# Parallel FNet and MLP on one core: a new order of the front, of four row stores and of one block's output columns

## The chip, the cores and the metric

The kernel runs on one core of one Trainium2 chip. The metric is the time of one execution on the device in microseconds (us), as the median of several runs. Before the change that is 851.08 us (three runs, 850.71 to 851.48). All matrices are 32-bit floats in and out.

## What is computed

For one sequence of S = 2048 rows and D = 640 columns, with F = 1536 hidden units:

```python
xn = _layernorm(x, axis=-1)
# _A_ref: real part of a Fourier transform along both axes
a = jnp.einsum("bsd,ed->bse", xn, dft_hid_re)
b = jnp.einsum("bsd,ed->bse", xn, dft_hid_im)
y = jnp.einsum("ts,bse->bte", dft_seq_re, a) - jnp.einsum("ts,bse->bte", dft_seq_im, b)
# _B_ref: a two-layer MLP
h = _gelu(jnp.einsum("bsd,df->bsf", xn, w1) + b1)
z = jnp.einsum("bsf,fd->bsd", h, w2) + b2
return x + y + z
```

## The kernel before, in words

**Products.** Every matrix product keeps nearly full precision by splitting both operands: a number is a high part, written by ScalarE as `fp32r` (L160), plus a low part, which VectorE computes as the difference (L161). One logical product is then three TensorE matmuls of 128x128 weights by 128x512 columns: high by high, high by low, low by high (L278 to L280, and L304 for the first layer of the MLP, where the three are the kinds `(0, 0)`, `(0, 1)`, `(1, 0)` of a chunk `j` of the 640 columns).

**Order.** The program is written out by hand: instructions stand on each engine in the order in which the code issues them, and nothing reorders them. An instruction whose input is late therefore holds all that stands behind it on its engine. DMAs are issued by SyncE (queue SP), by ScalarE (only the loads of two row chunks at the start, and the last stores) and by GpSimd (queue POOL).

**Stages.** The 2048 rows are four blocks of 512, each of four chunks of 128 rows. First the MLP of blocks 0 and 1: for each of 12 hidden units (of 128 columns) `hidden(g)` forms the hidden values in one PSUM bank, `gelu(g, acc)` activates and splits them, `output(g)` multiplies them by `w2` into five PSUM banks. `hidden` runs two units ahead of `output`. Beside it `first_block(i)` and `second_block(i)` normalize the later row chunks, store them to the scratch tensor `xs` in DRAM (`ln_apply`, L199 to L203), read them back by block (`load_z`) and turn them with VectorE; `prep_w` builds the Fourier weights and stores them to `wit` in DRAM from GpSimd's queue (L418). Then the MLP of blocks 2 and 3 runs with a scheme of sums that saves multiplications (`head`, `mid`, `finish`), then the Fourier transform.

**The front (L657 to L772).** The first four row chunks aren't normalized before their products: they are only centered, and the scale is multiplied in later. For chunk c, `x[c]` is loaded, its mean is found (VectorE's `ln_stats` for chunks 0 and 2, ScalarE's `sum_on_act` for 1 and 3), and `center` (L705, VectorE) or a ScalarE activation (L716, chunk 1) writes `xp[:, c]`. `transpose_x` (L693) turns 128x128 pieces of `xp` on TensorE into the PSUM banks `tacc[j]`, and `split` evicts each bank into `XTT` (tile `xtt`, high by ScalarE L160, low by VectorE L161). The weights of hidden unit 0 arrive in two pieces (columns 0 to 255 and 256 to 639) and are split at L728 and L729; those of unit 1 are loaded in two cuts of four DMAs each and split by `prep_w1(1)`. Before the transposes TensorE runs `NWARM` = 10 warm-up matmuls on a tile of zeros (L676), which VectorE clears (L665) and casts to `fp32r` (L667); one more stands between the transposes of chunks 1 and 2. `hidden(0)` takes its 15 matmuls in the order `FIRST`.

**The boundary after block 1 (from L1135).** The five output banks of block 1 are moved out by `outs`: for each of five column groups `e`, ScalarE adds the bias in the bank (L368), VectorE turns it into a scratch tile (L371), GpSimd adds it to the tile `xo` (L373). The banks so freed are what `mid(0)`, `head(1)` and `finish(0)` of the next stage need: `copy_bank` (L857) writes one of them, the bank sums (L452 on `banks` and `fifth`) two. `forms_s3` ends with a subtraction on `zs`, the split of one set of weight sums (`tw`), a load of the next, and one more form (`hs`), all ahead of `outs(1, (0,))`; `rest`, called inside `mid(0)` after its bank copy, moves out the other four column groups.

Of the kernel before, what the change touches and what calls it, by code (L numbers as in the profile page):

```python
# [15 lines left out]
P = 128  # L16
Q = 4
B = 32
EPS = 1e-5
NWARM = 10  # L20
# [6 lines left out]
def kernel(  # L27
# [171 lines left out]
    def ln_apply(c, eng=nc.vector):  # L199
        m = MV[:, c % 4]  # L200
        eng.tensor_scalar(xt[c], xt[c], m[:, 0:1], m[:, 3:4], op0=ALU.subtract, op1=ALU.mult)
        for k in range(NC):
            nc.sync.dma_start(xs[c % NC * NC + k, c // NC * B : (c // NC + 1) * B], xt[c][k * B : (k + 1) * B])  # L203
# [85 lines left out]

    def hidden(g, aside=None):  # L290
# [4 lines left out]
        if g == 0:  # L295
            steps = FIRST
        if g == 1:

            steps.sort(key=lambda s: s[1] == 2)
# [10 lines left out]
    FIRST = [(0, 0), (0, 2), (1, 0), (1, 2), (0, 1), (2, 0), (2, 2), (1, 1), (3, 0), (3, 2)]  # L310
    FIRST += [(2, 1), (4, 0), (4, 2), (3, 1), (4, 1)]
# [353 lines left out]
    nc.vector.memset(zeros, 0.0)  # L665
    warm = whole["as"][:, :TB]
    nc.vector.tensor_copy(warm, zeros)  # L667
# [3 lines left out]
    load_w1(1, cuts=(0, 2, ND))  # L671
# [3 lines left out]
    def warm_up():  # L675
        nc.tensor.matmul(wacc, warm[:, :P], warm, start=True, stop=True)  # L676
# [3 lines left out]
    load_w1(2)  # L680
# [41 lines left out]
    center(2, ALU.subtract, MV[:, 2, 0:1])  # L722
    sum_on_act(3)
    center(3, ALU.add, MV[:, 3, 5:6], 0, 2)
    center(3, ALU.add, MV[:, 3, 5:6], 2, ND)
    for lo, hi in ((0, 2 * P), (2 * P, D)):
        h, l = (W1[0][:, k, lo:hi] for k in range(2))
        nc.scalar.activation(h, first_w1[:, lo:hi], AF.Copy)  # L728
# [13 lines left out]
    acc0 = hidden(0)  # L742
    prep_w1(1)
    acc1 = hidden(1)
# [239 lines left out]
    def second_block(i):  # L984
# [8 lines left out]
        if i == 2:  # L993
            ln_scale(12, 4)
            for c in range(12, 16):
                ln_apply(c)
# [138 lines left out]
    outs(1, (0,), yt=lambda n: AB[:, 0], done=False)  # L1135
# [665 lines left out]
```

## Time and profile before

| what | us |
|---|---|
| median of three runs | 851.08 |
| the profiled execution | 850.46 |
| its span in the trace | 848.7 |
| TensorE busy in the span | 841.7 |
| VectorE busy | 666.8 |
| ScalarE busy | 356.0 |
| GpSimd busy | 48.9 |

The span runs from the first to the last instruction of the program; 1.76 us of the profiled execution lie around it. PE is TensorE's matmuls and PEld its weight loads, DVE is VectorE, ACT is ScalarE, POOL is GpSimd, SP is SyncE. A row of a timeline reads: start, duration, engine, line, operation, what is written from what is read with the shapes, count, and in brackets the idle time before it and what ended it. Matmuls overlap, so a matmul's duration is longer than the distance to the next one.

### The profile page before, as it was taken

How to read it: one execution, taken by the hardware profiler on the slowest of the kernel's cores; microseconds unless marked ns; L12 is line 12 of the kernel's file. 1: busy time of each engine (PE TensorE's matmuls, PEld its weight loads, DVE VectorE, ACT ScalarE, POOL GpSimd, SP SyncE). 2: the span in 40 equal slices, each digit the busy share in tenths (PEclk: the TensorE clock that was granted, in tenths of full speed). 3: DMA queues.
4: the chain of work that ended last, by engine and by line, in shares of the span. 5: the costliest groups of instructions: out<-in, count | busy, mean ns of one | idle time of the engine just before them, and what ended most of it. 6: DMA issues, size and time to landing. Idle time of an engine off the chain costs nothing.

```text
span 848.7 us, 10340 instructions
## 1 busy us (share of the span) xinstructions
PE 841.7 (99%) x3707; PEld 695.2 (82%) x3707; DVE 666.8 (79%) x841; ACT 356.0 (42%) x499; POOL 48.9 (6%) x70
## 2 busy tenths in 40 slices
PE   9999999999999999999999999999999999999997
PEld 7888888878888888888888888888888888888886
DVE  6665766776758888779988887889967898885687
ACT  7454534456665555343444344232323433223241
POOL 0000311031221400000000000000000000000001
PEclk9999999999999999999999999999999999999999
DMA  6667699837679989858644679663865779705464
GB/s 182 192 184 188 159 228 252 193 87 189 202 245 355 358 186 174 173 132 188 152 137 111 162 229 289 151 150 98 205 168 169 253 191 229 306 19 180 124 172 108
DMA packets 207491, 158.45 MB, mean 187 GB/s; under 512 B 81040, under 2 KB 180880, under 8 KB 206928
## 3 DMA queue, kind: packets, MB, share of 16 engines
q1 hardware_dynamic: 198752, 135.25, 62.7%
q0 software_dynamic: 4144, 21.24, 6.3%
q10 hardware_dynamic: 4544, 1.31, 0.6%
q8 instruction: 29, 0.48, 0.3%
q14 instruction: 22, 0.18, 0.1%
HBM read 114.76 MB, written 42.99 MB: 186 GB/s over the span
## 4 chain that ended last, share of the span: by engine, by line
PE 99%; DVE 0%; issue 0%
PE banks L278 29%; PE banks L279 29%; PE banks L280 29%; PE banks L304 10%; PE banks L676 1%; PE banks L693 0%; PE banks L336 0%; PE banks L339 0%; PE banks L337 0%; DVE yo L1766 0%; DVE zeros L665 0%; DVE as L667 0%; PE banks L764 0%
## 5 line engine op out<-in xcount | busy, mean ns | idle before, releaser
L278 PE MATMUL banks<-as,xab 128*128 128x512 f32 x411 | 159.9, 389 | 0.0
L280 PE MATMUL banks<-as,xab 128*128 128x512 f32 x411 | 159.9, 389 | 0.0
L279 PE MATMUL banks<-as,xab 128*128 128x512 f32 x411 | 159.9, 389 | 0.0
L160 ACT ACTIVATE as<-r 128x1024 fp32r<-128x1024 f32 x80 | 85.0, 1062 | 178.1 <-PE banks L280 149.7
L161 DVE TENSOR_TENSOR as<-r,as 128x1024 fp32r<-128x1024 f32 x80 | 97.2, 1216 | 41.5 <-ACT as L160 41.5
L278 PEld LDWEIGHTS banks<-as,xab 128*128 128x128 f32 x411 | 77.1, 188 | 16.1
L279 PEld LDWEIGHTS banks<-as,xab 128*128 128x128 f32 x411 | 77.1, 188 | 16.0
L280 PEld LDWEIGHTS banks<-as,xab 128*128 128x128 f32 x411 | 77.1, 188 | 16.0
L278 PE MATMUL banks<-as,xc 128*128 128x512 f32 x224 | 87.1, 389 | 0.0
L279 PE MATMUL banks<-as,xc 128*128 128x512 f32 x224 | 87.1, 389 | 0.0
L280 PE MATMUL banks<-as,xc 128*128 128x512 f32 x224 | 87.1, 389 | 0.0
L160 ACT ACTIVATE as<-rt 128x1024 fp32r<-128x1024 f32 x32 | 34.0, 1062 | 70.5 <-PE banks L280 62.5
L304 PE MATMUL banks<-xtt,xab 128*128 128x512 f32 x240 | 57.1, 391 | 0.0
L304 PEld LDWEIGHTS banks<-xtt,xab 128*128 128x128 f32 x240 | 44.7, 188 | 9.8 <-ACT xtt L160 0.4
L278 PEld LDWEIGHTS banks<-as,xc 128*128 128x128 f32 x224 | 42.0, 188 | 8.8
L279 PEld LDWEIGHTS banks<-as,xc 128*128 128x128 f32 x224 | 42.0, 188 | 8.7
L280 PEld LDWEIGHTS banks<-as,xc 128*128 128x128 f32 x224 | 42.0, 188 | 8.7
L161 DVE TENSOR_TENSOR as<-rt,as 128x1024 fp32r<-128x1024 f32 x32 | 38.8, 1211 | 5.3 <-ACT as L160 5.3
L160 ACT ACTIVATE as<-u 128x1024 fp32r<-128x1024 f32 (+1 forms) x24 | 22.1, 920 | 48.2 <-PE banks L280 48.2
L512 DVE STREAM_TRANSPOSE r<-raw 128x1024 f32<-128x1024 f32 x32 | 39.5, 1240 | 3.1 <-PE banks L280 2.6
L161 DVE TENSOR_TENSOR as<-u,as 128x1024 fp32r<-128x1024 f32 (+1 forms) x24 | 24.9, 1042 | 18.8 <-ACT as L160 18.8
L512 DVE STREAM_TRANSPOSE rt<-raw 128x1024 f32<-128x1024 f32 x32 | 38.8, 1230 | 0.9 <-PE banks L280 0.8
(352 smaller groups left out, 1618.5 us busy)
## 6 DMA issues: line engine op xcount, KB each, us to landing
raw<-in_A_dft_seq_re_dram SPq DMA_DIRECT2D x64, 256.0 KB, 5.6
raw<-in_A_dft_seq_im_dram SPq DMA_DIRECT2D x64, 256.0 KB, 5.0
ws<-wit SPq DMA_DIRECT2D x15, 384.0 KB, 5.4
xs<-x SPq DMA_DIRECT2D x64, 80.0 KB, 1.8
xo<-in_A_x_dram SPq DMA_DIRECT2D x16, 320.0 KB, 6.7
xab<-wit SPq DMA_DIRECT2D x13, 384.0 KB, 4.2
wit<-wstp POOLq DMA_DIRECT2D x12, 384.0 KB, 3.7
x<-in_A_x_dram SPq DMA_DIRECT2D x14, 320.0 KB, 4.4
```

What stands on the lines that cost most here:

```text
L160: nc.scalar.activation(h, s, AF.Copy)
L161: nc.vector.tensor_tensor(l, s, h.bitcast(F32), op=ALU.subtract)
L278: nc.tensor.matmul(acc, wh, mh, start=first, stop=False, skip_group_check=goes_on)
L279: nc.tensor.matmul(acc, wh, ml, start=False, stop=False, skip_group_check=goes_on)
L280: nc.tensor.matmul(acc, wl, mh, start=False, stop=last, skip_group_check=goes_on)
L304: nc.tensor.matmul(acc, W1[i][:, a, j * P : (j + 1) * P], XT[j][:, b], start=n == 0, stop=n == len(steps) - 1)
L512: nc.vector.transpose(held(pieces[g][2], u).rearrange("p c (n i) -> p c n i", i=B), r.rearrange("p n (c i) -> p c n i", i=B))
L676: nc.tensor.matmul(wacc, warm[:, :P], warm, start=True, stop=True)
```

## The change

**Warm-ups.** VectorE clears 128x128 zeros and casts nothing; 13 warm-ups of 128x128 by 128x128 in plain fp32 take the place of 10 of 128x512 in `fp32r`.

**The first transposes and products.** ScalarE, not VectorE, centers the first two column chunks of row chunk 3 (the fourth), before it takes the first weight piece. VectorE centers chunk 2 in two pieces (columns chunks 0 to 1, then 2 to 4). The second weight piece is split after the first two evictions. TensorE takes the last three transposes of chunk 3 after the first two products; `first_two` also interleaves the first matmuls of unit 1 with the last of unit 0. Unit 1's weights are loaded uncut, unit 2's in two cuts.

TensorE at the front (`as` and `zeros` are the warm-up tiles, `ident,xp` the transposes, `xtt,xab_122` and `xab_123` products of units 0, 1 and 2), before and now:

```order
L676 MATMUL banks<-as 128x512 x10
L693 MATMUL banks<-ident,xp 128x128 x10
L676 MATMUL banks<-as 128x512
L693 MATMUL banks<-ident,xp 128x128 x10
L304 MATMUL banks<-xtt,xab_122 128x512 x30
```

```order
L692 MATMUL banks<-zeros 128x128 x13
L709 MATMUL banks<-ident,xp 128x128 x10
L692 MATMUL banks<-zeros 128x128
L709 MATMUL banks<-ident,xp 128x128 x7
L304 MATMUL banks<-xtt,xab_122 128x512 x2
L709 MATMUL banks<-ident,xp 128x128 x3
L304 MATMUL banks<-xtt,xab_122 128x512 x28
```

Three transposes have moved behind two products; the number of transposes and products is the same.

ScalarE at the front, from the sum of chunk 3 (`ab,mv<-x_120`) to unit 1's weights (the last row of each), before and now:

```order
L699 ACTIVATE ab,mv<-x_120 128x640
L728 ACTIVATE xab_122<-w1r_139 128x256
L728 ACTIVATE xab_122<-w1r_139 128x384
L160 ACTIVATE xtt<-banks 128x512 x5
L160 ACTIVATE xab_122<-w1r_148 128x640
```

```order
L715 ACTIVATE ab,mv<-x_120 128x640
L745 ACTIVATE xp<-x_120,mv 128x4x2x32
L742 ACTIVATE xab_122<-w1r_138 128x256
L160 ACTIVATE xtt<-banks 128x512 x2
L742 ACTIVATE xab_122<-w1r_138 128x384
L160 ACTIVATE xtt<-banks 128x512 x3
L160 ACTIVATE xab_122<-w1r_147 128x640
```

One centering of 256 columns is new on ScalarE, and two evictions stand ahead of the second weight piece.

**Block 3's stores.** In `second_block(2)` the stores of chunks 12 and 13 go out from GpSimd's queue, those of 14 and 15 still from SyncE's.

**Block 1's columns.** The end of `forms_s3` becomes `forms_ob` and is called after `outs(1, (0,))`; column groups 2 and 1 are moved out before `mid(0)`, groups 3 and 4 still inside it. ScalarE at this boundary, from the two forms of `s3` to the two of `s4` (`b2c` marks the biases of `outs`, `banks<-banks` alone the bank copy of `mid(0)`), before and now:

```order
L160 ACTIVATE xtt<-zs 128x512 x2
L160 ACTIVATE tw_1549<-rq_1424 128x1024
L160 ACTIVATE hs<-zs 128x512
L368 ACTIVATE banks<-banks,b2c 128x512
L857 ACTIVATE banks<-banks 128x512
L368 ACTIVATE banks<-banks,b2c 128x512 x4
L160 ACTIVATE xtt<-zs 128x512 x2
```

```order
L160 ACTIVATE xtt<-zs 128x512 x2
L386 ACTIVATE banks<-banks,b2c 128x512
L160 ACTIVATE tw_1570<-rq_1427 128x1024
L160 ACTIVATE hs<-zs 128x512
L386 ACTIVATE banks<-banks,b2c 128x512 x2
L881 ACTIVATE banks<-banks 128x512
L386 ACTIVATE banks<-banks,b2c 128x512 x2
L160 ACTIVATE xtt<-zs 128x512 x2
```

The first bias is ahead of two splits, and two more are ahead of the bank copy. On VectorE the only move there is that the turn of the first column group (into `ab`) stands ahead of the subtraction on `zs`, the split of `tw` and the form in `hs`; the other four turns stay where they were.

The diff, cut to its core:

```diff
-NWARM = 10
+NWARM = 13
...
-    def ln_apply(c, eng=nc.vector):
+    def ln_apply(c, queue=nc.sync):
...
-            nc.sync.dma_start(xs[c % NC * NC + k, c // NC * B : (c // NC + 1) * B], xt[c][k * B : (k + 1) * B])
+            queue.dma_start(xs[c % NC * NC + k, c // NC * B : (c // NC + 1) * B], xt[c][k * B : (k + 1) * B])
...
+    def first_two():
+        kinds = ((0, 0), (0, 1), (1, 0))
+        second = sorted(((j, k) for j in range(ND) for k in range(3)), key=lambda s: s[1])
+        order = [(0, s) for s in FIRST[:13]] + [(1, s) for s in second[:2]]
+        order += [(0, FIRST[13]), (1, second[2]), (0, FIRST[14])] + [(1, s) for s in second[3:]]
+        for n, (g, (j, k)) in enumerate(order):
+            if n == 2:
+                transpose_x(3, 2, ND)
+                for e in range(2, ND):
+                    split(XT[e][:, 0], XT[e][:, 1], tacc[e])
+                prep_w1(1)
+            a, b = kinds[k]
+            ends = FIRST if g == 0 else second
+            nc.tensor.matmul(
+                bank(g),
+                W1[g][:, a, j * P : (j + 1) * P],
+                XT[j][:, b],
+                start=(j, k) == ends[0],
+                stop=(j, k) == ends[-1],
+            )
+        return bank(0), bank(1)
...
-    FIRST = [(0, 0), (0, 2), (1, 0), (1, 2), (0, 1), (2, 0), (2, 2), (1, 1), (3, 0), (3, 2)]
-    FIRST += [(2, 1), (4, 0), (4, 2), (3, 1), (4, 1)]
+    FIRST = [(0, 0), (0, 2), (1, 0), (1, 2), (0, 1), (2, 0), (1, 1), (3, 0), (2, 2), (3, 2)]
+    FIRST += [(4, 0), (4, 2), (2, 1), (3, 1), (4, 1)]
...
-    nc.vector.memset(zeros, 0.0)
-    warm = whole["as"][:, :TB]
-    nc.vector.tensor_copy(warm, zeros)
+    nc.vector.memset(zeros[:, :P], 0.0)
...
-    load_w1(1, cuts=(0, 2, ND))
+    load_w1(1)
...
-        nc.tensor.matmul(wacc, warm[:, :P], warm, start=True, stop=True)
+        nc.tensor.matmul(wacc[:, :P], zeros[:, :P], zeros[:, :P], start=True, stop=True)
...
-    load_w1(2)
+    load_w1(2, cuts=(0, 2, ND))
...
-    center(2, ALU.subtract, MV[:, 2, 0:1])
     sum_on_act(3)
-    center(3, ALU.add, MV[:, 3, 5:6], 0, 2)
-    center(3, ALU.add, MV[:, 3, 5:6], 2, ND)
-    for lo, hi in ((0, 2 * P), (2 * P, D)):
+
+    def split_first(lo, hi):
         h, l = (W1[0][:, k, lo:hi] for k in range(2))
         nc.scalar.activation(h, first_w1[:, lo:hi], AF.Copy)
         nc.vector.tensor_tensor(l, first_w1[:, lo:hi], h.bitcast(F32), op=ALU.subtract)
+
+    nc.scalar.activation(
+        chunked(xp[:, 3])[:, :, :2],
+        xt[3].rearrange("p (q c i) -> p q c i", q=Q, i=B)[:, :, :2],
+        AF.Identity,
+        bias=MV[:, 3, 5:6],
+    )
+    center(2, ALU.subtract, MV[:, 2, 0:1], 0, 2)
+    center(2, ALU.subtract, MV[:, 2, 0:1], 2, ND)
+    split_first(0, 2 * P)
+    center(3, ALU.add, MV[:, 3, 5:6], 2, ND)
     transpose_x(0, 0, ND)
     transpose_x(1, 0, ND)
     warm_up()
-    for j0, j1 in ((0, 2), (2, ND)):
-        transpose_x(2, j0, j1)
-        transpose_x(3, j0, j1)
-    for j in range(ND):
+    transpose_x(2, 0, 1)
+    transpose_x(3, 0, 2)
+    transpose_x(2, 1, ND)
+    for j in range(2):
         split(XT[j][:, 0], XT[j][:, 1], tacc[j])
+    split_first(2 * P, D)
...
-    acc0 = hidden(0)
-    prep_w1(1)
-    acc1 = hidden(1)
+    acc0, acc1 = first_two()
...
-                ln_apply(c)
+                ln_apply(c, nc.gpsimd if c < 14 else nc.sync)
...
+
+    def forms_ob():
         add(two(2), two(2), ZT, ALU.subtract)
         split_w1(1)
         load_rq(2)
...
     outs(1, (0,), yt=lambda n: AB[:, 0], done=False)
-
-    def rest():
-        free = (4, 5, 0, 1)
-        outs(1, (2, 1, 3, 4), yt=lambda n: A["zs"][:, free[n] * TB : (free[n] + 1) * TB])
-
+    forms_ob()
+    outs_at((2, 1), (4, 5))
     mid(0, rest)
```

`outs_at(order, free, done=False)` calls `outs(1, order, ...)` with scratch tiles `free` of `zs`, and the new `rest` is `outs_at((3, 4), (0, 1), done=True)`.

More of the change, by code (lines that the diff above doesn't have):

```diff
@@ L294, in hidden @@
         steps = [(j, k) for j in range(ND) for k in range(3)]
[L295 to L299, printed above, removed]
         for n, (j, k) in enumerate(steps):
@@ L1133, with outs_at, rest @@
     oacc[3] = [bank(k) for k in (5, 6, 7, 3, 4)]
+    def outs_at(order, free, done=False):
+        outs(1, order, yt=lambda n: A["zs"][:, free[n] * TB : (free[n] + 1) * TB], done=done)
+    def rest():
+        outs_at((3, 4), (0, 1), done=True)
     outs(1, (0,), yt=lambda n: AB[:, 0], done=False)
-    def rest():
-        free = (4, 5, 0, 1)
-        outs(1, (2, 1, 3, 4), yt=lambda n: A["zs"][:, free[n] * TB : (free[n] + 1) * TB])
+    forms_ob()
+    outs_at((2, 1), (4, 5))
     mid(0, rest)
```

2 lines of the change are left out of this document (1 added, 1 removed).

## Prediction

> **What bounds the kernel now.** I read the page first, then the chain that ended last, then the timeline of one engine at a time for the first 20 us and for 174 to 188 us.
>
> ```profile
> span 848.7 us, 10340 instructions
> PE 841.7 (99%) x3707; PEld 695.2 (82%) x3707; DVE 666.8 (79%) x841; ACT 356.0 (42%) x499; POOL 48.9 (6%) x70
> PE 99%; DVE 0%; issue 0%
> L278 PE MATMUL banks<-as,xab 128*128 128x512 f32 x411 | 159.9, 389 | 0.0
> ```
>
> TensorE is busy for 99% of the span and is 99% of the chain, and its groups have 0.0 us idle before them. An edit can therefore pay in two ways only: the products begin sooner, or a hole between products closes. TensorE in the front:
>
> ```profile
> 1.91 4.63 PE L676 MATMUL banks<-as 128*128 128x512 f32 x10 [1.91 <-DVE as L667]
> 6.42 1.98 PE L693 MATMUL banks<-ident,xp 128*128 128x128 f32 x10
> 8.16 0.48 PE L676 MATMUL banks<-as 128*128 128x512 f32 x1
> 8.48 1.25 PE L693 MATMUL banks<-ident,xp 128*128 128x128 f32 x10
> 9.66 7.46 PE L304 MATMUL banks<-xtt,xab 128*128 128x512 f32 x31
> 23.99 3.56 PE L304 MATMUL banks<-xtt,xab 128*128 128x512 f32 x15
> ```
>
> Ten warm-ups, ten transposes, a spare warm-up, ten transposes, then products from 9.66. A product in a full stream costs (3.56 - 0.39) / 14 = 0.226 us. The first 31 should take 30 x 0.226 + 0.39 = 7.17 and take 7.46, so waits inside them cost about 0.3.
>
> The speed of TensorE changes in the front (window, its length, PE busy and count, PEld, granted clock, DMA share, GB/s; line L693 alone):
>
> ```profile
> 6.40:7.70 1.30, 1.28 (x6) 1.30 (x7) 1.00 0.24 62
> 8.45:9.60 1.15, 1.12 (x10) 1.01 (x9) 1.00 0.28 72
> ```
>
> The same transpose takes 1.30 / 6 = 0.217 us before 7.7 and 1.15 / 10 = 0.115 after. The granted clock reads 1.00 in both, so the step is seen only in the spacing: TensorE reaches full speed about 5.8 us after its first matmul.
>
> **The front: what feeds the first product.** ScalarE, VectorE and the weight loads:
>
> ```profile
> 0.91 0.48 DVE L665 MEMSET zeros<- 128x512 f32 x1 [0.91 <-PEq L1787]
> 6.56 0.74 ACT L699 ACTIVATE ab<-x 128x640 f32<-128x640 f32 x1 [0.15 <-DMA x<-in_A_x_dram]
> 7.20 0.19 ACT L699 ACTIVATION_READ_ACCUMULATOR ab<-x 128x1 f32 x1
> 7.30 0.40 ACT L728 ACTIVATE xab<-w1r 128x256 fp32r<-128x256 f32 x1
> 7.38 1.15 DVE L705 TENSOR_SCALAR xp<-x,mv 128x640 f32<-128x640 f32 x3
> 8.47 0.53 ACT L728 ACTIVATE xab<-w1r 128x384 fp32r<-128x384 f32 x1 [0.77 <-DMA w1r<-in_B_w_dram]
> 9.01 2.56 ACT L160 ACTIVATE xtt<-banks 128x512 fp32r<-128x512 f32 x5
> 9.65 0.30 PEld L304 LDWEIGHTS banks<-xtt,xab 128*128 128x128 f32 x2 [0.16 <-ACT xtt L160]
> 12.42 0.74 ACT L160 ACTIVATE xab<-w1r 128x640 fp32r<-128x640 f32 x1 [0.86 <-DMA w1r<-in_B_w_dram]
> 13.21 3.48 PEld L304 LDWEIGHTS banks<-xtt,xab 128*128 128x128 f32 x16 [0.25 <-ACT xab L160]
> ```
>
> The first product waits for the first eviction (9.01, product at 9.66: 0.65 later). That eviction stands behind the second weight piece, for which ScalarE idles 0.77. The change moves that piece behind two evictions and gives ScalarE the first 256 columns of chunk four (a 128x256 activation, 0.40).
>
> *ScalarE's side.* Centering runs from 7.39 to 7.8, the first weight piece to 8.2, so an eviction can start at 8.25: a product at 8.9. On VectorE the three centerings of row 7.38 lose a quarter of their columns and wait behind one weight subtraction; they end near 8.9, before the three late transposes need them. The second piece then starts at 9.3, later than its landing at 8.47, and stream and evictions keep 0.1 us apart up to bank four. I cost it at nothing; the cover is those first six products, and a miss costs about 0.1.
>
> *TensorE's side.* The cast goes and the memset shrinks to a quarter. Its cost isn't shown: between 0.12 (a quarter of 0.48) and 0.48; I take 0.2, nearer the quarter, so warm-ups start at 1.15, not 1.91. There are 13 of fp32 128x128, a form that the trace lacks. The nearest rows are the slow fp32 transposes (0.217) and the slow 128x512 warm-ups ((6.42 - 1.91) / 10 = 0.45). I take 0.45, as the operation is a multiplication, not a transpose, and keep 0.217 for the range. The block then ends at 1.15 + 13 x 0.45 = 7.0: 0.6 *after* the chunk-0 transposes began before. The Trainium skill, "FP8 and Floating Point Precision", TensorE Precision Notes, says that true FP32 takes four passes through the array; four passes of 128 columns are the 512 of the old warm-up, which gives the 0.45 too, and no run here shows it yet.
>
> With full speed again 5.8 us after the first matmul (6.95): ten transposes at 0.115 to 8.15, the spare to 8.5, two transposes and their drain to 8.85, product 0.65 later at 9.5. The new order puts waits there: behind the first two products stand the last three transposes, and the evictions of banks two to four wait for those, so a late first product would hold them too. Three transposes (0.35) now stand inside the stream, so it stands where one begun at 9.85 would: 0.2 worse than 9.66. Against that, weights of block one come by four loads and not eight, and the wait at 13.21 (PEld 0.25, of which about 0.1 reaches PE, as a 0.19 load is partly covered) goes; fewer waits on the first evictions may give 0.1 more. Sum: 0.
>
> If full speed comes before about 5.5, the block ends in time, transposes start at 6.42 and run at 0.115 throughout: 7.6, the spare 7.9, two more and drain 8.25. That meets ScalarE's 8.25: product at 8.9, equivalent start 9.25, gain 0.4, plus 0.1 at 13.2: 0.5. The three timed runs of before lie 0.77 apart, as much as this whole difference, so I don't count on one fixed moment. I take **0.2** of 0 to 0.5. What is late next is ScalarE's chain of squares and spread; it starts with the weights of block one, which land sooner, and moves along.
>
> **The boundary at 174 to 188 us.**
>
> ```profile
> 174.26 1.29 DVE L161 TENSOR_TENSOR xtt<-zs,xtt 128x512 fp32r<-128x512 f32 x2 [0.88 <-ACT xtt L160]
> 178.34 0.71 DVE L371 STREAM_TRANSPOSE ab<-banks 128x512 f32<-128x512 f32 x1
> 179.15 0.58 ACT L857 ACTIVATE banks<-banks 128x512 f32<-128x512 f32 x1 [2.38 <-DVE ab L371]
> 179.49 0.39 PE L280 MATMUL banks<-xc,xab 128*128 128x512 f32 x1
> 179.78 0.50 PE L278 MATMUL banks<-xtt,tw 128*128 128x512 f32 x1
> 180.33 2.51 DVE L371 STREAM_TRANSPOSE zs<-banks 128x512 f32<-128x512 f32 x4 [1.28 <-ACT banks L368]
> 181.13 5.49 POOL L373 TENSOR_TENSOR xo<-xo,zs 128x512 f32<-128x512 f32 x4 [0.65 <-DVE zs L371]
> 182.77 1.26 DVE L452 TENSOR_TENSOR banks<-banks,fifth 128x512 f32<-128x512 f32 x2
> 183.79 0.39 PE L280 MATMUL banks<-r,tw 128*128 128x512 f32 x1
> 184.09 0.50 PE L278 MATMUL banks<-r,tw 128*128 128x512 f32 x1
> 183.94 3.23 DVE L161 TENSOR_TENSOR xtt<-zs,xtt 128x512 fp32r<-128x512 f32 x2
> 186.94 0.39 PE L278 MATMUL banks<-xtt,xab 128*128 128x512 f32 x1
> 187.22 0.50 PE L279 MATMUL banks<-xtt,xab 128*128 128x512 f32 x1
> ```
>
> Three holes. From 179.49 to 179.78 is 0.29, 0.06 over a step; that product lasts 0.50, not 0.39, as its weights couldn't load ahead, 0.11 more: 0.17 each, 0.51 in all. The first hole waits for the bank copy at 179.15, which waits for the transpose of 178.34, which stands on VectorE behind three long instructions. The change puts the transpose ahead of them and two bias activations ahead of the copy: copy ready near 178.8, hole closed, **0.17** sure.
>
> The second waits for the bank sums (182.77 to 184.03), the third for the forms from 183.94. The 1.28 idle before 180.33 goes, so the sums come 1.28 sooner, less what GpSimd's earlier add takes from VectorE. Price: two subtractions cost 1.29 alone and 3.23 beside GpSimd's adds (2.7 us of overlap), 0.72 per us; the moved add lasts 5.49 / 4 = 1.37: 1.0. Net 0.3 sooner, 183.7, while TensorE, 0.17 ahead, needs the sums at 183.85. Both holes close or stay by 0.1; half of 0.34 is **0.17**. The Trainium skill, "SBUF — State Buffer", SBUF: two separate sides, speaks against it: a GpSimd operation and a VectorE operation with two SBUF inputs exclude each other for a whole instruction. Its full block of one add would leave the sums at 184.0 and both holes open: 0.17 for the boundary in place of 0.34.
>
> **Block 3's stores.** Eight of sixteen go from SyncE to GpSimd.
>
> ```profile
> 128.61 0.54 POOL L418 DMA_DIRECT2D wit<-wst x1 [5.23 <-DVE wst L161]
> 132.72 10.72 SPq L203 DMA_DIRECT2D xs<-x  x16
> 136.77 1.34 ACT L160 ACTIVATE wst<-wt 128x256 fp32r<-128x256 f32 x4 [4.36 <-DVE wt L396]
> 154.45 1.25 DVE L786 STREAM_TRANSPOSE zt<-z 128x1024 f32<-128x1024 f32 x1 [2.88 <-DMA z<-xs]
> ```
>
> At 0.54 an issue they hold GpSimd 4.3 us, and the weight write of 128.61 stands behind them, some 2.5 us later. ScalarE reuses that buffer at 136.77 after 4.36 us of idle: covered, and without the cover ScalarE loses the excess, not TensorE, which has no hole there. SyncE is through 5 us sooner, and the 2.88 wait at 154.45 goes. TensorE didn't wait for it: **0**.
>
> **Rivals.** *A, full speed early:* the front gives 0.5, the boundary 0.34 to 0.51: 850.1 and below. The trace's 5.8 us speaks against, the spread for it. The Trainium skill, "TensorE: Matmul & The Clock Gate", Part 1, says that activity is judged in free-running windows of 3.4 us, so release moves from run to run; the 5.8 us fits. *B, no change:* the block holds the transposes, the front loses 0.2 to 0.4, the boundary gives it back: 851.1. For it: 7.0 against 6.42. *C, slower:* the 13 small matmuls cost more than 0.45, as each loads its own weights. Each 0.1 moves the front by 1.3; with half of the old block's 0.39 weight load uncovered (0.64 each) transposes start at 9.5, the front loses 2.7: 853.4. It passes 0.2% from about 0.57 each. Nothing shows such loads uncovered. *D, too short:* at 0.217 the block ends at 4.0, TensorE stands still for 2.4 us and products run slow to about 12.2 (6.42 + 5.8): half of 2.3 us and slow transposes, 1.5 lost, 852.3.
>
> **How the numbers follow.** The sum is -0.2 - 0.34 = -0.54. The profiled execution took 850.46 (span 848.7 plus 1.76 around it), which gives 849.9; the median of before is 0.62 above it, and on that footing the forecast is 851.08 - 0.54 = **850.5**. Chances: forecast (850.2 to 850.9) 0.48, A 0.2, B 0.2, C 0.06, D 0.06. The range runs from A's low end (849.5) to 852.1, short of C and part of D. 0.2%, about what a measurement can tell from no change, is 1.7 us: everything shown to be at stake is 0.5 + 0.51, so faster has 0.03, slower 0.06 (C, the top of D), the same 0.91.
>
> **What would show it.** Right: first warm-up near 1.15, ten transposes from 6.4 to 7.0, first product between 8.9 and 9.5, no PEld wait at the first product of block one, no hole near 179.8. Wrong: transposes starting after 7.2, products 0.43 apart after 10 us, holes still at 184.1 and 187.2, ScalarE idle on a weight write near 137, or any new hole in TensorE.

## The result, and the profile after

The changed kernel takes 852.87 us (median of 15 runs, 851.15 to 853.93), the kernel before beside it on the same chips 850.84 (15 runs, 850.3 to 851.7): a ratio of 1.0023, 95% interval 1.0016 to 1.003. It is slower by 2.0 us, where 850.5 and "the same" were forecast; 852.87 lies above the range. The profiled execution took 852.07 us, its span 850.3: 1.6 more than before.

The page of the profile after, in the order in which the lines of before were read (span, busy time with the number of instructions, chain by engine, the first group):

```profile
span 850.3 us, 10378 instructions
PE 842.7 (99%) x3724; PEld 696.8 (82%) x3724; DVE 666.6 (78%) x840; ACT 356.0 (42%) x500; POOL 54.0 (6%) x78
PE 86%; DVE 4%; DMA 3%; ACT 3%; SPq 2%; issue 2%; POOL 0%; ACTq 0%; POOLq 0%; DVEq 0%
L278 PE MATMUL banks<-as,xab 128*128 128x512 f32 x411 | 160.0, 389 | 0.5 <-DVE zs L389 0.5
```

TensorE's busy time rose by only 1.0, yet it is 86% of the chain where it was 99%: other engines now stand on the path for a part of the way. And there are 17 more matmuls and 17 more weight loads (x3724 for x3707), though the code issues only 3 matmuls more.

The front, TensorE's timeline of the kernel after; the last line is the first product of unit 0's output, and below it the same place before:

```profile
1.05 5.67 PE L692 MATMUL banks<-zeros 128*128 128x128 f32 x26 [1.05 <-DVE zeros L683]
6.56 1.25 PE L709 MATMUL banks<-ident,xp 128*128 128x128 f32 x10
8.94 0.73 PE L304 MATMUL banks<-xtt,xab 128*128 128x512 f32 x2
9.76 6.70 PE L304 MATMUL banks<-xtt,xab 128*128 128x512 f32 x28
20.19 0.39 PE L354 MATMUL banks<-hs,rt 128*128 128x512 f32 x1
```

```profile
20.59 0.39 PE L336 MATMUL banks<-hs,rt 128*128 128x512 f32 x1
```

The 13 fp32 warm-ups stand as x26: each is two instructions, about 0.21 us apart. The front does gain: at 20 us TensorE is 0.4 ahead (20.59 - 20.19). So the loss comes later. Two new groups of holes in TensorE, near 150 us and near 182 us:

```profile
148.32 1.29 PE L322 MATMUL banks<-xtt,as 128*128 128x512 f32 x5
149.82 0.50 PE L278 MATMUL banks<-hs,r 128*128 128x512 f32 x1 [0.20 <-ACT hs L344]
150.89 0.50 PE L279 MATMUL banks<-hs,r 128*128 128x512 f32 x1 [0.57 <-DVE hs L346]
151.23 0.39 PE L280 MATMUL banks<-hs,r 128*128 128x512 f32 x1
...
182.71 0.50 PE L278 MATMUL banks<-as,xab 128*128 128x512 f32 x1 [0.46 <-DVE zs L389]
```

With 0.226 a product, the five of 148.32 end their steps at 149.45; the next starts at 149.82, then 150.89, then 151.23: 0.37 + 0.84 + 0.11 = 1.3 us lost to the activation `hs`. Between 176 and 200 us the holes make 1.12 (0.73 of it at 182.71), before 0.52. The balance: -0.4 + 1.3 + 0.6 = 1.5 of the 1.6.

ScalarE makes `hs`. Its rows ahead of the hole, after, and the same activation before:

```profile
145.55 0.42 ACT L160 ACTIVATE wst<-wt 128x256 fp32r<-128x256 f32 x1 [3.41 <-DMA wit<-wst]
147.91 0.62 ACT L160 ACTIVATE wst<-wt 128x256 fp32r<-128x256 f32 x2 [1.74 <-DMA wit<-wst]
148.43 0.67 ACT L340 ACTIVATE ab<-banks,b1c 128x512 f32<-128x512 f32 x1
```

```profile
143.85 0.67 ACT L322 ACTIVATE ab<-banks,b1c 128x512 f32<-128x512 f32 x1
```

The activation is 4.6 us later, behind two waits for weight writes to DRAM. Going back along the engines, the first place where the two executions part is VectorE at 78 us. Before, then after:

```profile
78.63 0.71 DVE L238 STREAM_TRANSPOSE zt<-z 128x512 f32<-128x512 f32 x1 [0.60 <-DMA z<-xs]
105.75 0.89 DVE L185 BATCH_NORM_STATS2 st<-x 128x6 f32<-128x320 f32 x2 [0.54 <-DMA x<-in_A_x_dram]
```

```profile
79.48 0.71 DVE L238 STREAM_TRANSPOSE zt<-z 128x512 f32<-128x512 f32 x1 [1.79 <-DMA z<-xs]
107.02 0.89 DVE L185 BATCH_NORM_STATS2 st<-x 128x6 f32<-128x320 f32 x2 [2.22 <-DMA x<-in_A_x_dram]
109.08 0.89 DVE L185 BATCH_NORM_STATS2 st<-x 128x6 f32<-128x320 f32 x2 [0.92 <-DMA x<-in_A_x_dram]
```

VectorE reached the transpose 0.3 sooner and then waited 1.79 for the read of block 1's rows, not 0.60. SyncE issued that read 0.4 sooner (69.71, before 70.08), and its last quarter landed 9.6 us after the first issue (79.36), not 8.4 (78.51). The changed lines do not touch this read.

### The profile page after: what moved, and what is told of

Read it like the earlier page. It is cut to its first block, busy times and chain, and to the rows that moved or that the text cites. A ratio compares the mean times of both kernels' runs of the same rounds, so it can differ in the third digit from the quotient of the medians.

```text
span 850.3 us, 10378 instructions
## 1 busy us (share of the span) xinstructions
PE 842.7 (99%) x3724; PEld 696.8 (82%) x3724; DVE 666.6 (78%) x840; ACT 356.0 (42%) x500; POOL 54.0 (6%) x78
## 4 chain that ended last, share of the span: by engine, by line
PE 86%; DVE 4%; DMA 3%; ACT 3%; SPq 2%; issue 2%; POOL 0%; ACTq 0%; POOLq 0%; DVEq 0%
PE banks L279 27%; PE banks L278 27%; PE banks L280 27%; PE banks L322 3%; DMA wit<-wst 1%; DMA z<-xs 1%; PE banks L304 1%; SPq L406 1%; DMA xs<-x 1%; PE banks L692 1%; SPq L203 0%; ACT ab L340 0%; DVE r L161 0%; DVE zt L238 0%; DVE st L185 0%
## 5 line engine op out<-in xcount | busy, mean ns | idle before, releaser
L322 PE MATMUL banks<-xtt,xab 128*128 128x512 f32 x210 | 50.1, 390 | 0.0
L322 PEld LDWEIGHTS banks<-xtt,xab 128*128 128x128 f32 x210 | 39.3, 188 | 8.3 <-DVE xab L161 0.2
```

The source lines that it names most:

```text
L322: nc.tensor.matmul(acc, W1[i][:, a, j * P : (j + 1) * P], XT[j][:, b], start=n == 0, stop=n == len(steps) - 1)
```

## The experiments

All times are medians; "before" was run beside each group (850.66 to 850.79). The ratio is an estimate of its own with its interval and need not be the quotient of two medians. A profile shows one execution of a kernel, not its median.

| run | us | ratio to before, 95% |
|---|---|---|
| e1 stores only | 851.26 | 1.0006 (0.9997 to 1.0015) |
| e2 the change without the stores | 852.16 | 1.0019 (1.0011 to 1.0028) |
| e3 front only | 852.98 | 1.0031 (1.0019 to 1.0042) |
| e4 columns only | 850.60 | 1.0001 (0.9992 to 1.001) |
| e5 front, 5 long warm-ups | 850.40 | 0.9996 (0.9987 to 1.0004) |
| e6 before, 34 more instructions | 852.66 | 1.0018 (1.0009 to 1.0027) |
| e7 whole change, 5 long warm-ups | 850.87 | 1.0001 (0.9993 to 1.001) |
| e8 e7 without the stores | 850.16 | 0.999 (0.9982 to 0.9999) |
| e9 before, 34 more, later | 851.39 | 1.0007 (0.9999 to 1.0016) |
| e10 before, 110 more, small warm-ups | 856.22 | 1.0061 (1.0048 to 1.0073) |
| e11 e7, stores behind the weight writes | 849.93 | 0.9989 (0.998 to 0.9997) |
| e12 e7, later reads | 850.06 | 0.9992 (0.9983 to 1.0001) |
| e13 before, 5 products halved | 850.88 | 1.0003 (0.9994 to 1.0011) |
| e14 before, 11 halved | 852.13 | 1.002 (1.0011 to 1.0029) |
| e15 before, 17 halved | 853.00 | 1.0025 (1.0015 to 1.0035) |
| e16 before, 55 halved | 853.46 | 1.0022 (1.0012 to 1.0032) |

### Which part loses (e1 to e4)

e1, the stores alone (on the kernel before):

```diff
-                ln_apply(c)
+                ln_apply(c, nc.gpsimd if c < 14 else nc.sync)
```

> The kernel before with one edit: chunks 12 and 13 are stored to xs from GpSimd's queue. Theory W (weight writes): the stores push back GpSimd's weight writes to wit, ScalarE waits for their landing before it reuses the buffer, its activations of hidden values slip, and TensorE gets a hole near 150 us and late banks near 182: 1.5 to 2.6 us slower than before, holes only behind 149 us. Rival C (columns): the cost of the whole change sits in the new order at the boundary, and the stores alone cost under 0.5. Rival F (front): the front costs in most executions, the stores alone nothing.

e2, the change with this line put back:

```diff
-                ln_apply(c, nc.gpsimd if c < 14 else nc.sync)
+                ln_apply(c)
```

> The changed kernel with all of block 3's stores back on SyncE's queue. Theory W: the loss is gone and the front's gain is left, 0.2 to 0.8 under before, no hole near 150. Rival C: still 0.5 to 1.5 above before, with the hole near 182. Rival F: still 1 to 2 above before.

e3, the kernel before with the new front alone (warm-ups, centering, `first_two`, weight cuts). Against the whole change it takes back the line of e2, and at the boundary, where `forms_s3` gets the lines of `forms_ob` again and `rest` all four groups:

```diff
-    outs(1, (0,), yt=lambda n: AB[:, 0], done=False)
-    forms_ob()
-    outs_at((2, 1), (4, 5))
+    outs(1, (0,), yt=lambda n: AB[:, 0], done=False)
```

> The kernel before with the change's front alone. Theory W and rival C: 0.2 to 0.5 under before, the products from 8.9 us. Rival F: 1 to 2 above before, with the products later than 9.7 in the slower executions.

e4, the kernel before with the columns alone:

```diff
+    def forms_ob():
         add(two(2), two(2), ZT, ALU.subtract)
...
+    forms_ob()
+    outs_at((2, 1), (4, 5))
     mid(0, rest)
```

> The kernel before with the new order of block 1's columns alone. Theory W: 0.1 to 0.4 under before, the holes at 179.8, 184.1 and 187.2 (0.51 in all) down to 0.3 or less. Rival C: 0.5 to 1.5 above before, with a new hole of 0.7 or more near 181, where the next stage's first bank waits for a transpose that stands behind a split slowed by GpSimd's add. Rival F: no difference over 0.2.

The front alone loses 2.3 us; the stores alone 0.5, which the interval does not resolve; the columns nothing. So Theory W and Rival C are out as the main cause. Rival F has the right part but not the right way: in e3 the products begin as early as in the whole change (8.81), and its profile loses the time far behind them, 0.9 us near 136, 0.2 near 157 and 1.7 near 180 us.

Theory W's path exists, though. e1's profiled execution is its slowest (853.47 of 850.61 to 853.47), and in it TensorE has the hole of the changed kernel near 150 us, while VectorE's wait for the read at 70 us is that of before (0.59):

```profile
150.85 0.51 PE L278 MATMUL banks<-hs,r 128*128 128x512 f32 x1 [0.35 <-ACT hs L326]
151.93 0.50 PE L279 MATMUL banks<-hs,r 128*128 128x512 f32 x1 [0.57 <-DVE hs L328]
```

e2, with the late read and without the stores, has no hole there in its profile and loses 1.3 near 182 us. So the hole near 150 us comes with the stores; what the front alone costs shows near 180 us, and in e3 near 136 us too.

Why the columns gain nothing in e4 stands in its rows (VectorE, GpSimd, TensorE), with the split of `tw` before below them:

```profile
174.77 1.28 DVE L161 TENSOR_TENSOR xtt<-zs,xtt 128x512 fp32r<-128x512 f32 x2
177.71 2.31 DVE L161 TENSOR_TENSOR tw<-rq,tw 128x1024 fp32r<-128x1024 f32 x1
180.55 2.50 DVE L371 STREAM_TRANSPOSE zs<-banks 128x512 f32<-128x512 f32 x4
```

```profile
176.82 2.12 POOL L373 TENSOR_TENSOR xo<-xo,ab 128x512 f32<-128x512 f32 x1 [21.93 <-DVE ab L371]
```

```profile
181.30 0.50 PE L278 MATMUL banks<-as,xab 128*128 128x512 f32 x1
```

```profile
176.61 1.22 DVE L161 TENSOR_TENSOR tw<-rq,tw 128x1024 fp32r<-128x1024 f32 x1
```

The hole before `xtt,tw` is gone, but GpSimd's add now stands beside the split of `tw`, which takes 2.31 where it took 1.22. The four transposes start at 180.55 (before 180.33), and the first product on `as` at 181.30 waits for them: 0.06 and 0.11, a hole of the size of the one that was closed. The other two stay. Holes from 176 to 200 us: 0.56, before 0.52. But VectorE also came to this stretch later in e4: it begins the split into `xtt` at 174.77, before at 174.26. From there to the four transposes it took 5.78, before 6.07, so the new order is 0.29 quicker. In e7 below, with the same order at the boundary, VectorE came in time:

```profile
173.98 1.29 DVE L161 TENSOR_TENSOR xtt<-zs,xtt 128x512 fp32r<-128x512 f32 x2 [0.80 <-ACT xtt L160]
179.77 2.50 DVE L389 STREAM_TRANSPOSE zs<-banks 128x512 f32<-128x512 f32 x4
```

The holes from 176 to 200 us are 0.27 there, and 0.22 in the profiles of e11 and e12. So the columns do gain about 0.3 where VectorE isn't late; a median of e4 can't resolve that.

### What in the front loses (e5 to e8)

Nothing in the front touches the read at 70 us. What reaches it is TensorE's instruction stream. The page's section on DMA queues has a queue of its own for code; the line is the same before and after but for its share:

```profile
q8 instruction: 29, 0.48, 0.2%
```

29 packets of 16 KB, one about every 29 us, and TensorE has 2 x 3724 = 7448 instructions: 257 a packet. That they are TensorE's code is inferred from this, and from what follows. With 34 more instructions at the front every later fetch comes some 34 / 256 x 29 = 3.9 us sooner; the one that concerns us came 4.0 sooner (80.46, after 76.42). (The Trainium skill, "Runtime: NRT & Kernel Launch", Instruction fetch mechanics, says the same size: blocks of 16 KiB, 256 instructions, fetched by the sequencer's own DMA queue; the count agrees. It calls the cost of a crossing "mostly hidden": TensorE itself has no hole at this fetch, but the runs below show a cost to the transfer beside it.) The fetch of this queue before, in the window from 79.6 to 81.5 us, and after, from 76 to 78 us (packets, MB, share of 16 engines):

```profile
q8 instruction: 1, 0.02, 3.3%
```

```profile
q8 instruction: 1, 0.02, 4.3%
```

Before, it falls behind the read (landed 78.51); after, into it. *Theory I*: the fetch delays the transfer that it meets, and VectorE waits. e5 takes the new front (e3) but makes the warm-ups long and few, e7 does it to the whole change, e8 to the change without the stores:

```diff
-NWARM = 13
+NWARM = 5
...
-    nc.vector.memset(zeros[:, :P], 0.0)
+    nc.vector.memset(zeros[:, : 5 * P // 2], 0.0)
...
-        nc.tensor.matmul(wacc[:, :P], zeros[:, :P], zeros[:, :P], start=True, stop=True)
+        nc.tensor.matmul(wacc[:, :n], zeros[:, :P], zeros[:, :n], start=True, stop=True)
```

with `n` 320. e6 does the opposite: the kernel before, with 34 more instructions for the same columns (21 warm-ups of 256 for 10 of 512, and six products of unit 1 in two halves):

```diff
-NWARM = 10
+NWARM = 21
...
+            cuts = (0, TB // 2, TB) if g == 1 and 3 <= n < 9 else (0, TB)
```

> The front alone once more, but with 5 warm-ups of 128x320 in fp32 in place of 13 of 128x128: nearly the same time on TensorE and two TensorE instructions more than before the change, not 34 (each fp32 matmul shows as two). Theory I (instruction fetch): TensorE's code comes in blocks of 16 KB, one for each 256 instructions; 34 more instructions bring each block some 4 us earlier, into the last part of block 1's read (z) and the load of chunks 12 to 15, and everything that hangs on those is late at 180 us. Then this kernel is 0.2 to 0.6 under before, with a fetch near 80 us. Rival D (earlier weight loads): the front's earlier loads and products themselves collide with the reads; then it stays 1.5 to 2.5 above before, as the front alone did.

> The kernel before with 34 TensorE instructions more and the same work: 21 warm-ups of 128x256 in place of 10 of 128x512, and six products of hidden unit 1 cut into two halves of 256 columns. Theory I: 1.5 to 2.5 above before, a fetch near 76 us, the last part of block 1's read landing 9.4 to 9.8 us after its first issue and not 8.4. Rival D: within 0.4 of before, as no load moved.

> The whole change with 5 warm-ups of 128x320. Theory I: the stores' 0.5 and the front's gain are left, 850.5 to 851.4; rival D: 852.3 to 853.3, as the change.

> Front and block 1's columns without the stores on GpSimd, with 5 warm-ups of 128x320. Theory I: 0.3 to 0.8 under before, the best of all so far. Rival D: 1 to 2 above before, as the change without the stores.

All four times lie in Theory I's ranges and outside Rival D's. In e6's profile the fetch comes at 77.06 and the read's last quarter lands 9.6 us after the first issue, as asked. Each pair that differs in these instructions differs by about 2 us: e3 and e5 by 2.6, the whole change and e7 by 2.0, e2 and e8 by 2.0, e6 and the kernel before by 1.9. VectorE at 78 us in e5, then in e6:

```profile
78.36 0.71 DVE L238 STREAM_TRANSPOSE zt<-z 128x512 f32<-128x512 f32 x1 [0.35 <-DMA z<-xs]
```

```profile
79.93 0.71 DVE L238 STREAM_TRANSPOSE zt<-z 128x512 f32<-128x512 f32 x1 [1.75 <-DMA z<-xs]
```

So the loss belongs to the additional instructions, not to what the front computes: e6 has none of the change. e6's profiled execution was one of its quick ones (851.08 of 850.4 to 853.96): VectorE is late in it, and little of that reached TensorE (nothing up to 230 us, 0.4 behind it).

TensorE's five long warm-ups in e5, which the last part needs (x10, as each fp32 matmul shows as two):

```profile
1.25 5.70 PE L692 MATMUL banks<-zeros 128*128 128x320 f32 x10 [1.25 <-DVE zeros L683]
```

### Place of the fetch, or number of instructions? (e9, e10, e13 to e16)

e9 puts the same 34 behind the read, into the hidden units at 88 to 95 us; e10 puts 110 ahead of it, partly by small warm-ups:

```diff
+            cuts = (0, TB // 2, TB) if g == 12 and 3 <= n < 12 or g == 13 and 3 <= n < 11 else (0, TB)
```

```diff
-NWARM = 10
+NWARM = 32
...
-        nc.tensor.matmul(wacc, warm[:, :P], warm, start=True, stop=True)
+        nc.tensor.matmul(wacc[:, :n], warm[:, :P], warm[:, :n], start=True, stop=True)
...
+            cuts = (0, TB // 2, TB) if g in (1, 2, 3) and 3 <= n < 14 else (0, TB)
```

(`n` of the warm-ups is 160.)

> The kernel before, with the same 34 more instructions on TensorE as the sixth experiment, but later: 17 products of the hidden units at 88 to 95 us are taken in two halves of 256 columns. Theory I (a block of TensorE's code is fetched while the read of block 1's rows is under way, 70 to 78 us): here the fetch at 80.5 us stays where it is and only those from 108 us on come about 3.9 us sooner, so the last piece of that read lands 8.2 to 8.5 us after its issue as before, and the time is 850.4 to 851.2. Rival I-b (the later fetches, near 105 and 132 us, do the harm): last piece unchanged, time 852 to 853, holes between 135 and 190 us. Rival II (the number of instructions itself costs): 852 to 853 too, but with the lost time at the halved products.

> The kernel before, with 110 more instructions on TensorE for the same columns, all ahead of 28 us: 32 warm-ups of 160 columns for 10 of 512, and 33 products of hidden units 1 to 3 in two halves. The fetch of 80.5 us should come near 68 us, ahead of the read of block 1's rows (from 70.1 us), and the one of 135.7 near 123, inside the read of block 2's rows (121.7 to 130.7 us). Theory I (what counts is whether a fetch falls into a read, not how many instructions there are): the last piece of the first read lands 8.2 to 8.5 us after issue although there are three times as many extra instructions as in the sixth experiment; the last piece of the second read comes at 9.8 to 10.5 in place of 9.0; time 850.3 to 851.5 if that second read has slack, up to 852.5 if not. Rival II (each extra instruction costs): 856 or more, as the sixth experiment lost 1.9 with a third of them.

e9: the read's last piece comes 8.2 us after issue, and the time is 851.39, above the 851.2 that Theory I allowed and below what the rivals asked. Its interval (0.9999 to 1.0016) does not exclude that nothing changed. Most of the loss goes with the fetch near 77. About 0.26 of the 0.6 that is left is the price of the halved products themselves (two hidden units took 7.06, before 6.80); whether the later fetches cost the rest isn't settled. In e9's profile VectorE waits for the rows of chunks 12 to 15 (1.04 and 0.56) and TensorE has one hole of 1.1 at 180 us; but e5 has such waits too (1.89 and 0.79) and no such hole. VectorE in e9, then in e5:

```profile
106.42 0.89 DVE L185 BATCH_NORM_STATS2 st<-x 128x6 f32<-128x320 f32 x2 [1.04 <-DMA x<-in_A_x_dram]
108.11 0.89 DVE L185 BATCH_NORM_STATS2 st<-x 128x6 f32<-128x320 f32 x2 [0.56 <-DMA x<-in_A_x_dram]
```

```profile
106.98 0.89 DVE L185 BATCH_NORM_STATS2 st<-x 128x6 f32<-128x320 f32 x2 [1.89 <-DMA x<-in_A_x_dram]
108.91 0.89 DVE L185 BATCH_NORM_STATS2 st<-x 128x6 f32<-128x320 f32 x2 [0.79 <-DMA x<-in_A_x_dram]
```

e10 was a poor experiment: its time is set by its own warm-ups.

```profile
1.91 7.11 PE L682 MATMUL banks<-as 128*128 128x160 f32 x32 [1.91 <-DVE as L673]
```

In this slow phase 160 columns cost 7.11 / 32 = 0.22, as much as 256 in e6, so the block ends at 8.8 and the first output product comes at 23.50, 2.9 late. The time, 856.22, is what Rival II asked; but the profile is of the fastest execution (853.97), so where the others lose 2 us more isn't shown. Only the milestone counts: the fetch at 67.8 lies ahead of the read, whose last piece takes 8.6 in spite of 110 more instructions.

e13 to e16 leave the warm-ups alone and halve 5, 11, 17 and 55 products (10, 22, 34 and 110 instructions) of the first units. The condition in `hidden`, one line each:

```diff
+            cuts = (0, TB // 2, TB) if g == 1 and 3 <= n < 8 else (0, TB)
+            cuts = (0, TB // 2, TB) if g == 1 and 3 <= n < 14 else (0, TB)
+            cuts = (0, TB // 2, TB) if g == 1 and 3 <= n < 14 or g == 2 and 3 <= n < 9 else (0, TB)
+            cuts = (0, TB // 2, TB) if 0 < g < 6 and 3 <= n < 14 else (0, TB)
```

> The kernel before, with five products of hidden unit 1 in two halves (10 more instructions, about 1.1 us of TensorE's stream). The fetch of 80.5 us comes near 79.4, still behind the read of block 1's rows (issue 70.1, last piece 78.5). Theory I (the place of the fetch counts): last piece 8.2 to 8.6 us after issue, time 850.4 to 851.1. Rival II (the number of instructions counts, 1.9 us for 34): about 851.3.

> The kernel before, with eleven products of unit 1 in two halves (22 more instructions). The fetch comes near 78.0, at the very end of the read. Theory I: last piece between 8.4 and 9.6 us, time anywhere from 850.6 to 852.6, the later the piece the longer. Rival II: about 852.0.

> The kernel before, with 17 products of units 1 and 2 in two halves (34 more instructions, as many as the change adds, none of them a warm-up). The fetch comes near 76.6, inside the read. Theory I: last piece 9.4 to 9.8 us, time 852 to 853, as the sixth experiment. Rival II: 852.7 as well. If the time is that of before, the loss belongs to the warm-ups after all.

> The kernel before, with 55 products of units 1 to 5 in two halves (110 more instructions). The fetch comes near 68, ahead of the read of block 1's rows; the one of 135.7 comes near 123, inside the read of block 2's rows (121.7 to 130.7). Theory I: the last piece of the first read 8.2 to 8.6 us, and TensorE has no more than 0.5 us of new holes up to 170 us; time 850.6 to 851.8, depending on whether the second read has slack. Rival II: 856.9.

The fetch came at 79.8, 79.2, 77.6 and 66.3 us, and the times are 850.88, 852.13, 853.00 and 853.46. Theory I *as stated* fell in e15: the read's last piece took 8.1 us (8.4 in e14), undisturbed, and the kernel lost 2.3 us all the same. VectorE's rows say why. In order, e13 and e14 and e15:

```profile
78.38 0.71 DVE L238 STREAM_TRANSPOSE zt<-z 128x512 f32<-128x512 f32 x1 [0.37 <-DMA z<-xs]
79.01 0.88 DVE L185 BATCH_NORM_STATS2 st<-x 128x6 f32<-128x320 f32 x2
80.06 0.83 DVE L185 BATCH_NORM_STATS2 st<-x 128x6 f32<-128x320 f32 x2
```

```profile
79.66 0.89 DVE L185 BATCH_NORM_STATS2 st<-x 128x6 f32<-128x320 f32 x2
81.60 0.89 DVE L185 BATCH_NORM_STATS2 st<-x 128x6 f32<-128x320 f32 x2 [0.81 <-DMA x<-in_A_x_dram]
```

```profile
78.50 0.71 DVE L238 STREAM_TRANSPOSE zt<-z 128x512 f32<-128x512 f32 x1 [0.26 <-DMA z<-xs]
80.47 0.89 DVE L185 BATCH_NORM_STATS2 st<-x 128x6 f32<-128x320 f32 x2 [1.26 <-DMA x<-in_A_x_dram]
```

Behind the read stand the loads of chunks 8 to 11, and VectorE takes their statistics one after the other. A fetch at 76 to 77 meets the last piece of the read, one at 77.6 chunk 8, one at 79.2 chunk 9: each time VectorE waits about a microsecond more, on the very transfer that was landing. At 79.8 or later it meets chunks 10 and 11, whose statistics VectorE takes only at 90.7, and nothing is lost (e13, and the kernel before with 80.5). The landings agree. The read's last quarter lands 1.4 us behind the third before, and 2.8 behind it in the changed kernel and in e6; chunk 8 is the late one in e15, chunk 9 in e14, chunk 10 in e13 and chunk 11 before. Amended, the theory is: the fetch delays by 1.2 to 1.5 us *whatever transfer it meets*, and it costs what goes beyond the time that the reader of that transfer has in hand.

e16's time failed too, but not in this way. TensorE in its profile is 1.5 behind by 46 us: 0.6 because the transposes start late (7.02, before 6.42; e1, with the front of before, starts products 0.3 late too), the rest mostly the halved products. It keeps that distance to 200 us, without a hole near 180, and loses 0.5 near 206 and 1.1 near 285 us, for reasons that were not followed. Its fetch at 66.3 does meet a transfer, the stores of chunks 4 to 7, and SyncE's issues of these sixteen took 8.71 us in e16 (first line), 7.36 before; what that cost TensorE isn't shown:

```profile
62.80 8.71 SPq L203 DMA_DIRECT2D xs<-x  x16
```

```profile
61.27 7.36 SPq L203 DMA_DIRECT2D xs<-x  x16
```

Rival II, a price for each instruction, is out as the main cause: by the medians 10 cost 0.2, 22 cost 1.5, 34 cost 2.3 and 110 cost 2.8, not 7.6; and 34 placed later cost 0.6. e14 and e15 alone would fit it (852.0 and 852.7 were asked). A small price there is. Unit 2 in e16, with 11 of its 15 products halved, took 0.15 more than the 3.56 that its 15 whole ones took from 23.99 before:

```profile
25.00 3.71 PE L306 MATMUL banks<-xtt,xab 128*128 128x512 f32 x26
```

So 55 halved products cost about 0.7 us of e16's 2.8, and 17 about 0.2 of e15's 2.3.

### The stores (e11, e12)

e7 and e8 differ by the stores alone: 850.87 (849.89 to 852.84) and 850.16 (849.77 to 850.33). GpSimd's rows in e7:

```profile
125.80 4.31 POOL L203 DMA_DIRECT2D xs<-x  x8 [3.32 <-DVE x L201]
131.08 1.65 POOL L436 DMA_DIRECT2D wit<-wst  x3 [0.97 <-DMA xs<-x]
```

The three weight writes stand behind the eight stores, and the last of those waits for a store to land. S1 says that this costs; S2 that SyncE, relieved of eight stores, starts the next read 4 us sooner (139.75, in e8 143.84), into the weight writes. e11 issues the eight stores behind the writes; e12 puts the reads one step later, with VectorE's last turn of the block before:

```diff
-                ln_apply(c, nc.gpsimd if c < 14 else nc.sync)
+                ln_scaled(c)
+            for c in (14, 15):
+                ln_store(c, nc.sync)
...
+            if i == 2:
+                for c in (12, 13):
+                    ln_store(c, nc.gpsimd)
```

```diff
-            turn_z1(ZT[:, 0], 4)
-            load_z(3)
         if i == 4:
             form_of("a11", 0, two(0)[:, 0], lane("as", 5))
-            open_xf()
         if i == 5:
+            turn_z1(ZT[:, 0], 4)
+            load_z(3)
+            open_xf()
```

(`ln_scaled` is the scaling of `ln_apply`, `ln_store` its four DMAs.)

> The whole change with five warm-ups of 320 columns (850.87 in the seventh experiment, 850.16 without the stores on GpSimd), and the eight stores on GpSimd issued behind the weight writes of the same step, not ahead of them. Theory S1 (the weight writes wait behind the stores in GpSimd's queue): 850.1 to 850.5, and the weight writes of that step land within 4.5 us. Theory S2 (with half of the stores gone from SyncE the next read starts 5 us sooner, into the weight writes): 850.7 to 851.2, as in the seventh.

> The whole change with five warm-ups of 320 columns, and the reads of block 3's rows and of the first weight sums put one step later in SyncE's order. Theory S1 (weight writes behind the stores): 850.7 to 851.2, no better than the seventh experiment. Theory S2 (the earlier read collides with the weight writes): 850.1 to 850.5.

Each came out on the side of its own theory and against the other, a little under the ranges: 849.93 with the early read kept (140.21), 850.06 with the writes still behind the stores. Taken together, neither alone costs anything that shows; the two at once do, 0.7 to 0.9 us by the medians, an amount near the width of the intervals. The traces show the two meeting. In e1 and in the changed kernel two weight writes leave with the read (141.65 and 141.63; 140.53 and 140.64) and land after 4.9 to 6.7 us, and both have the hole near 150 us. In e7's profile, one of its quick ones, they leave 2.0 us ahead of it and land after 2.9 and 4.0. GpSimd in e11, writes first:

```profile
129.84 1.07 POOL L442 DMA_DIRECT2D wit<-wst  x2 [1.11 <-DVE wst L161]
130.90 3.98 POOL L205 DMA_DIRECT2D xs<-x  x8
```

e11 is the fastest kernel of the case: 0.9989 of before, interval 0.998 to 0.9997; the whole change, with few warm-ups and the stores behind the writes.

## Why the prediction was wrong, by its own steps

- **The warm-ups' time: right.** 0.45 each was forecast, 2 x 0.213 = 0.427 came; 7.0 for the end of the block, 6.6 came. A slow `fp32r` warm-up of 512 columns costs 0.427 as well (before, e9). That alone shows little, as in this phase 160 columns cost 0.213 too (e10); but in e5 320 columns of fp32 take 2 x 0.533, per column 4.0 times as much as the `fp32r` warm-up. So the four passes that the Trainium skill names ("FP8 and Floating Point Precision", TensorE Precision Notes) are now borne out.
- **The front's gain: right in mechanism, low in size.** First product at 8.94, no wait at unit 1's first product, 0.4 gained of "0.2 of 0 to 0.5". Rival A's reason came true: full speed came 5.3 us after the first matmul, not 5.8. The size has luck in it, for that moment moves from execution to execution: in the profiles it came 3.5 to 5.8 us after the first matmul with the old front (e15, before) and 3.9 to 5.3 with the new (e3, after). The first output product came at 20.59 to 21.14 with the old (before, e1, e4, e9), at 20.04 to 20.23 with the new (after, e2, e3).
- **"13 of fp32 128x128" priced by time alone: the step that failed.** The sum counted what TensorE does with the warm-ups and not that they are instructions. They are 26, with 26 weight loads; 34 more than before in all. That moved a fetch of code by 4.0 us into a transfer, and cost 2 us (e5 to e8).
- **"What is late next": wrong.** The text named ScalarE's chain of squares, which "moves along". Late next was VectorE, on a read that the change does not touch. The argument "an edit can pay in two ways only" rested on TensorE being 99% of the chain; a second chain, from the read at 70 us over VectorE, SyncE's stores and loads, GpSimd's weight writes and ScalarE to the products near 180 us (near 150 us only with the stores), stood less than about a microsecond behind, and a chain of waits shows only the one that ended last.
- **The boundary, 0.34: right in mechanism, but nothing came in the changed kernel.** "Net 0.3 sooner" is what the order gives: 6.07 from the split to the four transposes before, 5.78 and 5.79 in e4 and e7. VectorE lost 1.09 to GpSimd's add, for which 1.0 was priced. In e7, e11 and e12 the holes fell from 0.52 to between 0.22 and 0.27, the first gone and 0.1 to 0.2 left of each of the others. The sum took for granted that VectorE comes there in time. In e4 it came 0.5 later, in the changed kernel 1.9 (176.17), and the gain was gone. The rule of the Trainium skill ("SBUF — State Buffer", SBUF: two separate sides) that such instructions exclude each other fits e4's rows: the subtraction on `zs` ends at 177.79, the add at 178.94, the split at 180.02, one behind the other. The time worked out beside it, sums at 184.0 and both holes open, did not come where VectorE was in time: in e7 the sums end at 183.45, with TensorE 0.28 ahead.
- **The stores, 0, "covered": wrong by 0.5 to 0.7.** ScalarE does wait on weight writes (3.41 and 1.74 above), and the cover of 4.36 at 136.77 was not the one that counted: the harm came with the next writes, together with the earlier read (e1, e7, e11, e12). "SyncE is through 5 us sooner" was counted as a gain.
- **The rivals.** C and D priced slow small matmuls wrongly for this change. A floor for small matmuls does show elsewhere (e10: 160 columns cost as much as 256); whether weight loads set it, as C thought, no run shows. No rival had a delay outside the front, so the chance of slower, 0.06, was far too small.

Still open: which of the 16 DMA engines carries the fetch, and so why it holds up just one piece; whether the fetches near 105 and 132 us cost anything; and why one microsecond at VectorE becomes one to two at TensorE, and in e6's profile none up to 230 us. The way from 80 to 180 us was followed in the rows, not cut by an experiment. Runs of the kernels that lose also spread over 2 to 4 us, those of e8 over 0.6.

## What to carry to other kernels

Count instructions as well as time: where an engine's code is fetched in blocks by DMA while data moves (here 16 KB for 257 instructions), a few dozen more instructions at the start move every later fetch, and an unrelated transfer may be late 60 us on. A chain of waits that is 99% one engine does not say how far behind the next chain stands; look for waits on DMAs that end just in time, and ask what 1 us there would do. And when a queue is relieved, ask what it will now start sooner.

## What the runs showed of the hardware

- A plain fp32 matmul is two matmul and two weight-load instructions in the trace (x26 for 13).
- One 16 KB fetch of code, itself 1.0 to 1.4 us long in before, after, e6 and e13 to e15, delayed the transfer that was landing by 1.2 to 1.5 us.
- In the slow phase a matmul of 160 columns and one of 256 cost the same, 0.213 us (e10, e6). At full speed 11 products in two halves cost 0.15 us more than whole ones (e16).
- TensorE reached full speed 3.5 to 5.8 us after its first matmul, from one execution of the same warm-ups to another (e15, before).
